# Linear attention and a two-layer MoE block on one core: seven chunk pairs by block products instead of four, weights streamed from DRAM, a recorded instruction order

## The chip, the cores and the metric

The kernel runs on one core of one Trainium2 chip. The metric is the device time of one execution in microseconds (us), median of several runs. The engines are named as the profile names them: PE (TensorE, matmuls), PEld (its weight loads), DVE (VectorE), ACT (ScalarE), POOL (GpSimd) and SP (SyncE, which issues nearly all DMAs from one queue, in order).

## The reference

```python
# q, k, v: (8, 8, 576, 64); w_phi: (64, 128); w_in: (512, 2048); w_out: (2048, 512)
def phi(x):
    proj = np.einsum('bhsd,df->bhsf', x, w_phi)
    proj = proj - np.max(np.abs(proj), axis=-1, keepdims=True)
    return np.concatenate([np.exp(proj), np.exp(-proj)], axis=-1)
q_p, k_p = phi(q), phi(k)
kv = np.einsum('bhsf,bhsd->bhfd', k_p, v)
z = np.sum(k_p, axis=2)                       # the key sums
num = np.einsum('bhsf,bhfd->bhsd', q_p, kv)
den = np.einsum('bhsf,bhf->bhs', q_p, z)[..., None] + 1e-06
x = (num / den).transpose(0, 2, 1, 3).reshape(4608, 512)
h = np.maximum(x @ w_in, 0.0)
out = (h * h) @ w_out
```

## The kernel before

**Attention.** The 64 heads are handled as 32 pairs of heads. The first six pairs (`early`) run while the weights are prepared; the other 26 go through a pipeline of visits (`visit(i)`, `late(p)`): one visit projects the queries of pair i and the keys of pair i+1, makes K'V of pair i and the numerators of pair i-1. The largest absolute projection of each query and the denominators are reduced over partitions by POOL (`partition_all_reduce`, four per pair). The key sums z are made by DVE in `keys` and `late`: per head one add of halves (512 columns), one add of quarters (256) and one add of the last 64 tokens (256), then per pair a 32x32 block transpose and a reduction (512 each). The result makes a round trip through DRAM (`zd`, `za`).

**MoE.** The 4608 tokens are 18 chunks of 256. The hidden layer is cut into 8 pieces of 256 columns (f), so a chunk takes 8 steps. A step has a first matmul (x times w_in, f16 in two halves, three products per block), relu and squaring on ACT, a split of the square into a high and a low part (`gh`, `gl`; the last subtraction on DVE), and a second matmul with w_out of 12 matmuls with 512 columns. The first matmul of one chunk is 24 matmuls of 256 columns (`moe`, line 1051). Chunks 0 to 9 are done so, mixed into the attention.

**Block products.** The last eight chunks are done as four pairs (`pair`, line 1233): for two chunks at once the product is cut into 2x2 blocks and made with seven block products in place of eight (Strassen's scheme in Winograd's form): 42 matmuls of 256 columns where two ordinary first matmuls have 48. Its price is on DVE: sums of weight blocks (`add_w`), sums of chunk blocks (`add_x`), and in each step four adds on the products in PSUM (line 1248: three of 512 columns, one of 256). In the first pair three of the eight steps are ordinary ones, so 29 steps are block steps. w_in lies in SBUF throughout (`win`), and a ring of seven chunk places holds x; chunks 10 to 12 are spilled to DRAM and read back.

**Order.** Every operation is an entry of a plan with its engine, cost, predecessors, buffers and rank. A list scheduler (`Plan.order`, with ranks from a table) computes when each would start and writes the program out in that order; an operation that may run on several engines goes to the one that is free first. At run time each engine runs its own list in order and waits on semaphores.

Of the kernel before, what the change touches and what calls it, by code (L numbers as in the profile page):

```python
# [37 lines left out]
RING = 7 * T  # L38
# [7 lines left out]
LEAD = 36.0  # L46
STEP = 1.4
EARLY = 6
BANKS = 5
STAY = 6.0  # L50
LATER = 2.0
BEHIND = 0.0
MOVED = 70.0
CHANGE = 0.18
RA, RQ, RZ = 1.3, 0.4, 0.3
WARM = 8
FILL_TO = 125.0
PAIRED = 10
PLAIN = 3
SPILLED = (10, 11, 12)  # L60
PAIRS = ((13, 14), (15, 16), (17, 10), (11, 12))
TAIL = LEAD + (STEP - 1.0) * PAIRED * NFP

# [22 lines left out]
class Plan:  # L86
# [11 lines left out]
    def __init__(self):  # L98
        self.ops = []
        self.bufs = {}  # L100
        self.single = set()

# [8 lines left out]
    def close(self):  # L111
# [18 lines left out]

        for (tag, n), mine in users.items():
            if tag in self.single:
                first = mine[0]
                first.after += [a for op in mine[1:] for a in op.after if a not in mine and not self.leads(first, a)]
        self.users = {key: len(mine) for key, mine in users.items()}

    def leads(self, first, op):
        seen, todo = set(), [op]
        while todo:
            x = todo.pop()  # L140
            if x is first:
                return True
            for a in x.after:
                if a.n not in seen:
                    seen.add(a.n)
                    todo.append(a)
        return False

    def improve(self):

        some = [op for op in self.ops if -50.0 < op.rank < MOVED]
        assert 2 * len(some) == len(RANKS)
        for n, op in enumerate(some):
            i, j = (DIGITS.index(x) for x in RANKS[2 * n:2 * n + 2])
            op.rank = (90 * i + j - 3000) * 0.05
        return self.order()

    def order(self):
        for op in self.ops:
            op.start = op.end = None  # L160
            op.next, op.left = [], 0
            op.after = [a for a in {id(a): a for a in op.after}.values() if a is not op]
            op.behind = [a for a in op.behind if a not in op.after and a is not op]
        for op in self.ops:
            for a in op.after + op.behind:
                a.next.append(op)
                op.left += 1
# [8 lines left out]
        def alone(op):  # L176
            return [key for key in op.uses if key[0] in self.single]
# [13 lines left out]
        for op in self.ops:  # L191
            if not op.left:
                release(op)
# [1248 lines left out]
```

## Time and profile before

| | before |
|---|---|
| time, median of 3 runs | 1020.16 us (1019.26 to 1021.61) |
| span of the profiled execution, first to last instruction | 1018.5 us |
| PE busy | 999.8 us (98%) |
| DVE busy | 763.2 us (75%) |
| ACT busy | 680.5 us (67%) |
| POOL busy | 361.2 us (35%) |
| moved by DMA | 77.34 MB, mean 76 GB/s |

The profiled execution is known by its span alone: 1018.5 us, 1.7 us under the median of the runs, and what lies around the span is taken as those 1.7 us. A busy PE is read with care, since matmuls overlap: the time that one costs is read from the distance of starts, not from its length.

### The profile page before, as it was taken

To read this page: it belongs to the slowest core of one execution; us is meant where nothing else is said; L and a number is where in the kernel's file an instruction comes from. 1 tells how busy PE (TensorE), PEld (TensorE's weight loads), DVE (VectorE), ACT (ScalarE), POOL (GpSimd) and SP (SyncE) were. 2 spreads that over 40 slices of the span, in tenths; PEclk is the share of its full clock that TensorE was granted. 3 is DMA by queue.
4 is the path that set the end of the run, shared out by engine and by line. 5 is a ranking of instruction groups with operands and counts; after the bars stand their busy time and mean duration, and the time that the engine had idled before them with its cause. 6 is when DMAs were issued, how large, how long until landed. Compare 5 with 4: busy or idle time off the path is not lost.

```text
span 1018.5 us, 19261 instructions
## 1 busy us (share of the span) xinstructions
PE 999.8 (98%) x7632; PEld 694.6 (68%) x7713; DVE 763.2 (75%) x1221; ACT 680.5 (67%) x1206; POOL 361.2 (35%) x138
## 2 busy tenths in 40 slices
PE   8999999999999999999999999999999999999998
PEld 4657776776666667666767666666776767677675
DVE  5899878798878989777879888798888447343432
ACT  6989886777777787686777867776555445435444
POOL 2433356364456555475375646563000000000000
PEclk9999999999999999999999999999999999999999
DMA  9754323132322233233324212110002001000001
GB/s 355 282 186 135 122 81 94 39 110 73 85 60 81 75 93 93 60 82 81 107 80 111 83 48 69 41 41 22 13 2 83 1 1 49 14 1 21 22 1 42
DMA packets 94914, 77.34 MB, mean 76 GB/s; under 512 B 58088, under 2 KB 72424, under 8 KB 92776
## 3 DMA queue, kind: packets, MB, share of 16 engines
q1 hardware_dynamic: 94536, 75.59, 24.6%
q8 instruction: 60, 0.98, 0.4%
q10 hardware_dynamic: 288, 0.52, 0.1%
q14 instruction: 30, 0.25, 0.1%
HBM read 61.16 MB, written 14.78 MB: 75 GB/s over the span
## 4 chain that ended last, share of the span: by engine, by line
PE 90%; DVE 3%; DMA 3%; ACT 2%; issue 1%; SPq 0%; DVEq 0%; ACTq 0%
PE po L1088 27%; PE ph L1051 21%; PE pp L1233 7%; PE pz L669 4%; PE pv L1088 4%; PE pn L1088 4%; PE ph L1233 3%; PE pn L904 3%; PE pn L884 2%; PE pp L611 2%; PE pv L904 2%; PE pz L1233 2%; PE pz L674 1%; PE pv L669 1%; PE pz L892 1%
## 5 line engine op out<-in xcount | busy, mean ns | idle before, releaser
L1051 PE MATMUL ph<-ring,win 128*128 128x256 f16 x2064 | 240.4, 273 | 0.8 <-ACT r L1060 0.8
L1051 PEld LDWEIGHTS <-win 128*128 128x128 f16 x2064 | 195.3, 98 | 47.0 <-issue 24.8
L982 POOL PARTITION_ALL_REDUCE mx<-pt x52 | 121.6, 2339 | 122.7 <-ACT pt L335 84.3
L1088 PE MATMUL po<-wh,gh 128*128 128x512 f32 x448 | 143.8, 442 | 0.0
L1003 POOL PARTITION_ALL_REDUCE rb<-rb x26 | 96.5, 3712 | 112.0 <-DVE rb L1000 95.6
L1265 ACT ACTIVATE qe<-qe,cw 128x512 f32<-128x512 f32 x58 | 41.4, 715 | 112.5 <-DVE qe L1248 112.5
L1088 PE MATMUL po<-wl,gl 128*128 128x512 bf16 x448 | 115.1, 379 | 0.0
L331 DVE TENSOR_TENSOR gl<-r,gh 128x512 bf16<-128x512 f32 x86 | 87.5, 1018 | 31.7 <-ACT r L1070 30.7
L1003 POOL PARTITION_ALL_REDUCE ds<-ds x26 | 98.7, 3797 | 25.2 <-DVE ds L1000 24.5
L1088 PE MATMUL po<-wl,gh 128*128 128x512 bf16 x375 | 101.5, 379 | 4.9 <-issue 1.6
L1088 PEld LDWEIGHTS <-gl 128*128 128x128 bf16 x576 | 56.4, 98 | 68.0
L1088 PEld LDWEIGHTS po<-wh,gh 128*128 128x128 f32 x448 | 84.6, 189 | 25.9
L1248 DVE TENSOR_TENSOR qe<-pp,qe 128x512 f32<-128x512 f32 (+1 forms) x87 | 52.3, 602 | 61.3 <-PE pp L1233 59.5
L1060 ACT ACTIVATE r<-ph,cw 128x512 f32<-128x512 f32 x86 | 58.7, 683 | 51.0 <-PE ph L1051 49.3
L331 DVE TENSOR_TENSOR gl<-qe,gh 128x512 bf16<-128x512 f32 x58 | 40.1, 691 | 65.7 <-ACT qe L1070 65.6
L1088 PEld LDWEIGHTS <-gh 128*128 128x128 bf16 x576 | 52.3, 98 | 50.7 <-issue 8.9
L633 ACT ACTIVATE e<-e 128x512 f32<-128x512 f32 x64 | 40.0, 625 | 32.3 <-DVE e L630 32.3
L1233 PEld LDWEIGHTS <-win 128*128 128x128 f16 x522 | 48.8, 98 | 14.2 <-issue 7.8
L1068 ACT ACTIVATE gh<-r 128x512 fp32r<-128x512 f32 x86 | 54.1, 629 | 5.7 <-PE pv L1088 2.0
L1070 ACT ACTIVATE r<-r 128x512 f32<-128x512 f32 x86 | 54.3, 631 | 2.7
L650 DVE TENSOR_TENSOR es<-e 128x512 f32<-128x512 f32 x52 | 46.3, 890 | 4.5 <-ACT e L635 4.3
L669 PE MATMUL pz<-e,v 128*64 128x256 f32 x416 | 49.3, 379 | 0.0
(286 smaller groups left out, 1970.4 us busy)
## 6 DMA issues: line engine op xcount, KB each, us to landing
v<-in_vp_dram SPq DMA_DIRECT2D x32, 320.0 KB, 4.1
k<-in_kp_dram SPq DMA_DIRECT2D x32, 288.0 KB, 4.1
q<-in_qp_dram SPq DMA_DIRECT2D x32, 288.0 KB, 3.4
rb<-rd SPq DMA_DIRECT2D x64, 144.0 KB, 3.1
out_dram<-o SPq DMA_DIRECT2D x34, 256.0 KB, 2.1
td<-kvs SPq DMA_DIRECT2D x26, 128.0 KB, 2.6
kz<-td SPq DMA_DIRECT2D x26, 128.0 KB, 2.9
spill<-ring SPq DMA_DIRECT2D x6, 256.0 KB, 2.9
```

The costliest lines, as they stand in the source:

```text
L331: eng.tensor_tensor(out=out_, in0=a, in1=b_, op=ALU.subtract)
L669: PE.matmul(out=to[64 * h:64 * h + 64, 0:256], lhsT=v_[p][:, t, h, :], rhs=e_[2 * p + h][:, t].rearrange("p s f -> p (s f)"), start=t == 0 ...
L904: PE.matmul(out=to[64 * h:64 * h + 64, :], lhsT=kz_[n][:, 128 * s_ + 64 * h:128 * s_ + 64 * h + 64], rhs=qe_[2 * n + h].rearrange("p (s x) ...
L982: o = P.add("POOL", par_us(S), lambda n=n, h=h: G.partition_all_reduce(mx_[n], pt_[p][:, h, :], channels=128, reduce_op=bass_isa.ReduceOp. ...
L1003: o = P.add("POOL", 3.6, lambda y=y: G.partition_all_reduce(y(), y(), channels=128, reduce_op=bass_isa.ReduceOp.add), [o], [home], R(RQ + ...
L1051: PE.matmul(out=ph[:, j, :], lhsT=win[w][:, t, 128 * ff:128 * ff + 128], rhs=at_ring(c, x, t), start=k == 0, stop=k == 3 * KT - 1)
L1060: o = P.add("ACT", act_us(512, 1), lambda: A.activation(out=r_[n], in_=ph_[bank], func=AF.Relu, scale=cw[:, f, 0:1]), [g1], [("ph", bank), ...
L1068: sq = P.add("ACT", act_us(512), lambda: A.activation(out=gh_[n], in_=r(), func=AF.Square), after, use + [("gh", n)], Q)
L1070: o = P.add("ACT", act_us(512), lambda: A.activation(out=r(), in_=r(), func=AF.Square), [sq], use, Q, other=[("DVE", 0.70, lambda: V.tenso ...
L1088: PE.matmul(out=bank(i), lhsT=x[:, j, 128 * i:128 * i + 128], rhs=w[:, j, :], start=turn + j + s == 0, stop=(turn, j, s) == (NFP - 1, 1, 2))
L1233: PE.matmul(out=to, lhsT=fl(x, *al)(k), rhs=fr(y, *ar)(k), start=n == 0, stop=n == 5)
L1248: V.tensor_tensor(out=to, in0=a, in1=b, op=ALU.add)
```

## The change

1. **Seven pairs.** Chunks 0 to 3 stay ordinary; chunks 4 to 17 are seven pairs, each with eight block steps (`step`). That is 56 block steps in place of 29 and 32 ordinary first matmuls in place of 86.
2. **w_in streamed.** Once scaled, the pieces of w_in are stored to DRAM (`wd`), and so are the sums of their blocks, which are made once, early (`ahead`). Each block step loads its piece and its block sums again, 0.5 MB each, into one of two buffers (`weights`). The room in SBUF goes to the temporaries, and the ring has eight places; nothing is spilled.
3. **One of two chunks put away.** In the first six pairs the step's second matmul is made for the first chunk alone. `gh` and `gl` of the second chunk go to DRAM (`put_away`) and are read back for eight second matmuls after the pair's steps (`take_back`). Those steps use the PSUM banks pn and pv, which the attention uses too.
4. **Key sums.** Per head one DVE reduction over 1024 columns with `apply_transpose`, and per pair one over 256; the results go through DRAM and one more small reduction. The subtraction for the last 64 keys moves from DVE into two ACT activations with a bias.
5. **Order.** Ranks and scheduler are gone. A table `ORDER` holds the place of each operation and a string `WAYS` the engine of those that have a choice; the code still computes start times, which now only place the filling matmuls.

```diff
-RING = 7 * T
+RING = 8 * T
-PAIRED = 10
-PAIRS = ((13, 14), (15, 16), (17, 10), (11, 12))
+PAIRED = 4
+PAIRS = [(c, c + 1) for c in range(PAIRED, NCH, 2)]
+MID = 6
...
     def order(self):
+        assert 2 * len(self.ops) == len(ORDER)
+        place = {}
         for op in self.ops:
...
+            place[op.n] = 90 * i + j
+        several = [op for op in self.ops if len(op.ways) > 1]
+        for op, way in zip(several, WAYS, strict=True):
+            op.take(list(op.ways)[int(way)])
+        order = sorted(self.ops, key=lambda op: place[op.n])
...
-        for h in range(0 if p < EARLY else 2):
-            n = 2 * p + h
-            o = P.add("DVE", dve_us(512), lambda n=n: V.tensor_tensor(
-                out=es_[p][:, 512:1024], in0=e_[n][:, 0:2].rearrange("p t s f -> p (t s f)"),
-                in1=e_[n][:, 2:4].rearrange("p t s f -> p (t s f)"), op=ALU.add),
...
+            def fold(src, col, k, after, use, rank):
+                sums[p].append(P.add("DVE", dve_us(256 * k), lambda: V.tensor_reduce(
+                    out=col(), in_=src().rearrange("p k (b x) -> p k b x", x=32), op=ALU.add, axis=AX.X, apply_transpose=True),
+                    [after], [use, ("z4", p)], rank))
...
+    def weights(f, rank):
+        b = in_pair["step"] = in_pair.get("step", 1) ^ 1
+        o = P.add("SP", 0.45, lambda: SP.dma_start(wo_at(b), wd_[f][0]), [w_stored[f]] + read_o[b], [WO[b]], rank, land=2.4, xfer=1.8)
+        if f in s_stored:
+            s = P.add("SP", 0.45, lambda: SP.dma_start(ws_at(b).rearrange("p k n x c -> p k (n x c)"), wd_[f][1]), s_stored[f] + read_s[b], [WS[b]], rank, land=2.4, xfer=1.8)
+            read_o[b], read_s[b] = [], []
+            return b, [o, s]
...
+    def step(cs, k, turn, f, n, m):
...
+        b, w_ready = weights(f, m - 5.0)
...
+        pa = P.add("PE", 0.66, lambda: product(banks[0]()[:, 0, :], "a11", "b11"), after, keys[0] + reads, m)
...
+        pb = P.add("PE", 1.31, two(1, ("a12", "b21"), ("s2", "t2")), [pa], keys[1] + reads, m + 0.01)
+        cb_ = P.add("DVE", dve_us(512), lambda: plus(r()[:, 0:4:3, :], banks[1](), wide(r()[:, 1, :])), [ca, pb], keys[1] + [rt], Q - URGENT)
+        pc = P.add("PE", 1.31, two(2, ("s3", "t3"), ("s1", "t1")), [pb], keys[2] + reads, m + 0.02)
...
+        pd = P.add("PE", 1.31, two(3, ("a22", "t4"), ("s4", "b22")), [pc], keys[3] + reads, m + 0.03)
+        cd = P.add("DVE", dve_us(512), lambda: plus(r()[:, 1:3, :], banks[3](), r()[:, 1:3, :]), [pd, c22], keys[3] + [rt], Q - URGENT)
...
+    def put_away(n, k, f, g, rank):
+        def work():
+            SP.dma_start(gd_[k % 2][f][0], gh_[n].bitcast(F32))
+            SP.dma_start(gd_[k % 2][f][1], gl_[n])
...
+        for j in range(NFP):
+            done = step(cs, k, j, j, n, m)
+            second(n, cs[0], v, j, j, done[0], m + 2.5, po)
+            if mid:
+                put_away(n + 1, k, j, done[1], m)
             else:
-                for i in range(2):
-                    n = v * NFP + 2 * j + i
-                    moe(cs[i], f, j, n, TAIL + n, po[i])
+                second(n + 1, cs[1], v + 1, j, j, done[1], m + 3.5, later)
```

In a block step the bank `ph` holds the first of the seven products and, as a second tile, the last two; the copy `ca` and the add `cd` free it.

The order on DVE, before, for one attention pair in the middle of the program. The es rows are the key sums (three adds per head, transpose, reduction), e the exponentials of the keys, gl the low part of a square.

```order
L655 TENSOR_TENSOR es_3627<-es_3627 128x256
L660 TENSOR_TENSOR es_3627<-es_3627,et_3662 64x256
L650 TENSOR_TENSOR es_3627<-e_3618 128x512
L331 TENSOR_TENSOR qe_3699<-pt_3592,mx_3660 128x576
L655 TENSOR_TENSOR es_3627<-es_3627 128x256
L660 TENSOR_TENSOR es_3627<-es_3627,et_3662 64x256
L1000 SCALAR_TENSOR_TENSOR rb_3721<-qe_3651,zc_3519,pp_3701 128x576
L966 STREAM_TRANSPOSE es_3627<-es_3627 128x512
L331 TENSOR_TENSOR gl_3727<-r_3716,gh_3719 128x512
L967 TENSOR_REDUCE z_8_3757<-es_3627 128x4x4
```

And after the change, at a like place. L1167 are the adds on the products in PSUM (pn, pv, ph) of block steps, w_1 the two temporaries of a step, L580 the new key sums.

```order
L1167 TENSOR_TENSOR w_1_4086<-pv_4254,w_1_4086 128x512
L1167 TENSOR_TENSOR w_1_4086<-pv_4254,w_1_4086 128x256
L1167 TENSOR_TENSOR w_1_4086<-ph_4273,w_1_4086 128x512
L877 STREAM_TRANSPOSE kvs_4317<-pz_4292 128x256
L249 TENSOR_TENSOR gl_4319<-w_1_3621,gh_4271 128x512
L570 TENSOR_REDUCE kmt_4334<-pz_4292 128x1
L249 TENSOR_TENSOR gl_4354<-w_1_3621,gh_4290 128x512
L1167 TENSOR_TENSOR w_1_3621<-pn_4337,w_1_3621 128x2x256
L1167 TENSOR_TENSOR w_1_3621<-pv_4356,w_1_3621 128x512
L1167 TENSOR_TENSOR w_1_3621<-pv_4356,w_1_3621 128x256
L580 TENSOR_REDUCE z_9_4235<-e_3458 128x2x4x4
```

The adds of the key sums have left DVE's list, and adds that read PSUM stand among the attention's operations, which before they did only after the attention's end.

SP's list before, in the later part of the attention: small transfers of the attention (den, rd, rb, td, kz, zd, za) and loads of q, k and v.

```order
L1005 DMA den_5848<-rb_5791 64x1x9
L971 DMA zd_5855<-z_16_5850 128x16
L972 DMA za_5873<-zd_5855 128x4x4
L1005 DMA den_5848<-ds_5832 64x1x9
L821 DMA rd_5909<-rc_5905 128x9
L604 DMA q_5924<-in_qp_dram 128x576
L603 DMA k_5928<-in_kp_dram 128x576
L566 DMA v_5934<-in_vp_dram 128x640
L954 DMA td_5936<-kvs_5930 128x2x128
```

And after the change, at a like place. `wd` are the streamed weights and their block sums, `gd` the parts that are put away.

```order
L1091 DMA w_1_3921<-wd_0_88 128x2048
L1093 DMA w_1_4026<-wd_1_89 128x2048
L524 DMA k_6869<-in_kp_dram 128x576
L1223 DMA gd_0_0_98<-gh_6783 128x512
L1224 DMA gd_0_1_99<-gl_6871 128x512
L878 DMA td_6898<-kvs_6888 128x2x128
L890 DMA zd_6914<-z_17_6758 128x72
L881 DMA kz_6962<-td_6898 128x8x32
L754 DMA rb_6527<-rd_6804 64x576 x2
```

The streamed loads and the parts put away now stand in the same queue as the attention's small transfers. The order also gives the counts that the prediction uses. On PE, 768 rows of ordinary first matmuls are left of 2064, and the block products grow from 1218 to 2352; second matmuls (1728) and attention keep their counts. On SP, 112 loads of 0.5 MB are added, and 96 transfers each way for what is put away.

## Rows read from the trace of the kernel before

**Rows 1.** The page, parts 1 and 2: busy time, and busy tenths in 40 slices.

```profile
PE 999.8 (98%) x7632; PEld 694.6 (68%) x7713; DVE 763.2 (75%) x1221; ACT 680.5 (67%) x1206; POOL 361.2 (35%) x138
DVE  5899878798878989777879888798888447343432
```

**Rows 2.** Windows: us, busy us (and instructions) of each engine, granted clock, DMA.

```profile
83.00:703.00 620.00, 616.15 (x4766) 429.71 (x4813) 525.70 (x828) 461.95 (x839) 331.54 (x114) 1.00 0.29 80
703.00:1014.00 311.00, 307.78 (x2015) 217.82 (x2046) 171.91 (x271) 148.06 (x237) 3.40 (x1) 1.00 0.05 19
```

**Rows 3.** Waits of PE from 83 us on: us in total, times, longest.

```profile
PE po L1088 <- issue: 1.6, 10, 0.2
PE pp L1233 <- DVE qe L1248: 0.9, 1, 0.9
PE ph L1051 <- ACT r L1060: 0.8, 1, 0.8
```

**Rows 4.** Timeline of PE, two places: start us, us, what.

```profile
87.40 2.79 PE L1051 MATMUL ph<-ring,win 128*128 128x256 f16 x24
90.03 1.03 PE L1088 MATMUL po<-wl,gh 128*128 128x512 bf16 x3
...
92.69 0.50 PE L1051 MATMUL ph<-ring,win 128*128 128x256 f16 x3
...
722.39 0.83 PE L1233 MATMUL pz<-ring,win 128*128 128x256 f16 x6
...
729.64 0.83 PE L1233 MATMUL pz<-ring,win 128*128 128x256 f16 x6
```

**Rows 5.** Groups of DVE instructions, all shapes apart: busy us, mean ns, idle before.

```profile
L650 DVE TENSOR_TENSOR es<-e 128x512 f32<-128x512 f32 x52 | 46.3, 890 | 4.5 <-ACT e L635 4.3
L655 DVE TENSOR_TENSOR es<-es 128x256 f32<-128x256 f32 x52 | 39.0, 750 | 1.1
L660 DVE TENSOR_TENSOR es<-es,et 64x256 f32<-64x256 f32 x52 | 33.4, 643 | 1.8
L966 DVE STREAM_TRANSPOSE es<-es 128x512 f32<-128x512 f32 x26 | 18.4, 707 | 0.4
L967 DVE TENSOR_REDUCE z<-es 128x16 f32<-128x512 f32 x26 | 17.8, 683 | 0.5
L640 DVE TENSOR_TENSOR et<-pz,kmt 128x128 f32<-128x128 f32 x26 | 7.4, 286 | 0.7
L331 DVE TENSOR_TENSOR gl<-r,gh 128x512 bf16<-128x512 f32 x86 | 87.5, 1018 | 31.7 <-ACT r L1070 30.7
L1248 DVE TENSOR_TENSOR qe<-pp,qe 128x512 f32<-128x512 f32 x58 | 40.0, 690 | 60.3 <-PE pp L1233 59.5
L1248 DVE TENSOR_TENSOR qe<-pp,qe 128x256 f32<-128x256 f32 x29 | 12.3, 424 | 1.0
L1000 DVE SCALAR_TENSOR_TENSOR rb<-qe,zc,pp 128x576 f32<-128x576 f32 x26 | 21.0, 807 | 1.1 <-ACT pp L998 0.8
```

**Rows 6.** Lines 331 and 1003 alone: min/median/max ns, first and last start.

```profile
L331 DVE TENSOR_TENSOR gl<-r,gh x86: 650/692/3050, 89.0 to 722.2; 128x512 bf16<-128x512 f32 x86
L331 DVE TENSOR_TENSOR gl<-qe,gh x58: 680/692/694, 731.5 to 1008.8; 128x512 bf16<-128x512 f32 x58
...
L1003 POOL PARTITION_ALL_REDUCE rb<-rb x26: 3592/3593/4123, 146.6 to 696.9; - x26
```

**Rows 7.** DVE's busiest 20 us in the attention, from windows.

```profile
380.00:400.00 20.00, 19.95 (x158) 13.82 (x158) 19.58 (x31) 14.13 (x26) 11.78 (x5) 1.00 0.31 86
```

**Rows 8.** DMA issues: KB each, median us from issue to landing.

```profile
raw7i<-in_w_in_dram SPq DMA_DIRECT2D x1, 1024.0 KB, 4.8
raw4i<-in_w_in_dram SPq DMA_DIRECT2D x1, 1024.0 KB, 11.0
```

**Rows 9.** SP's own waits, 83 to 703 us.

```profile
SPq L1005 <- POOL rb L1003: 91.4, 23, 8.2
```

More of the change, by code (lines that the diff above doesn't have):

```diff
@@ L129, in close @@
                 op.after.append(first)
[L131 to L134, printed above, removed]
         self.users = {key: len(mine) for key, mine in users.items()}
[L137 to L156, printed above, removed]
     def order(self):
+        assert 2 * len(self.ops) == len(ORDER)
+        place = {}
         for op in self.ops:
[L160 to L167, printed above, removed]
+            i, j = (DIGITS.index(x) for x in ORDER[2 * op.n:2 * op.n + 2])
+            place[op.n] = 90 * i + j
[3 more added lines that the diff above has]
+        order = sorted(self.ops, key=lambda op: place[op.n])
         free = dict.fromkeys(self.HOP, 0.0)
-        waiting = {e: [] for e in self.HOP}
-        ready = {e: [] for e in self.HOP}
-        holder, open_at, parked = {}, {}, {}
+        holder, open_at = {}, {}
         mode, moved = WHOLE, 0.0
@@ L174, in order @@
         users = dict(self.users)
-        def alone(op):
-            return [key for key in op.uses if key[0] in self.single]
-        def release(op):
-            least = max([open_at.get(tag, 0.0) for tag, n in alone(op) if holder.get(tag) != n] + [a.start + 0.001 for a in op.behind], default=0.0)
-            for eng in op.ways:
-                at = least
-                for a in op.after:
-                    at = max(at, a.there + (self.HOP[a.eng] if a.eng != eng or a.land else 0.0))
-                second = eng != next(iter(op.ways))
-                heapq.heappush(waiting[eng], (at + LATER * second, op.rank + BEHIND * second, op.n))
@@ new lines, in order @@
+        for op in order:
+            e, (us, _, lock) = op.eng, op.ways[op.eng]
+            op.start = max([free[e]] + [a.there + (self.HOP[a.eng] if a.eng != e or a.land else 0.0) for a in op.after if a is not op]
+                           + [a.start + 0.001 for a in op.behind if a is not op])
+            alone = [key for key in op.uses if key[0] in self.single]
+            for tag, n in alone:
+                assert holder.get(tag, n) == n
+                if tag not in holder:
+                    op.start = max(op.start, open_at.get(tag, 0.0))
+            op.end = op.start + us
@@ L229, in order @@
                 else:
-                    op.end += min(lock, max(0.0, locked["POOL"] - t))
+                    op.end += min(lock, max(0.0, locked["POOL"] - op.start))
                     locked[e] = op.end
@@ L1351, in tile_kernel @@
     pool_next.after += pool_prep
+    ring1.after += [op for op in P.ops if v_key(NP) in op.uses]
     for op in P.ops:
@@ L1375, in tile_kernel @@
         if free:
-            fills.append((t0, len(P.ops), lambda tag=free[0], n=n, count=int(0.6 * (t1 - t0) / 0.214): zeros(tag, n, count)))
+            fills.append((t0, lambda tag=free[0], n=n, count=int(0.6 * (t1 - t0) / 0.214): zeros(tag, n, count)))
     with tc.manual_schedule():
-        for _, _, fn in sorted([(op.start, op.n, op.fn) for op in order] + fills, key=lambda x: x[:2]):
-            fn()
+        for op in order:
+            while fills and fills[0][0] <= op.start:
+                fills.pop(0)[1]()
+            op.fn()
```

679 lines of the change are left out of this document (361 added, 318 removed).

## The prediction, made before the changed kernel ran

> **What bounds the kernel now.** I read the page's busy times first, then windows, then PE's waits. PE is busy for 98% of the span [rows 1], so the question is where it is not. Three stretches answer it: until the first first-matmul (83 us), the attention with ordinary chunks (83 to 703), and the pairs (703 to 1014). In the second PE is busy for 616 of 620 us, in the third for 308 of 311, at a full granted clock [rows 2]; all its named waits behind 83 us come to 3.3 us [rows 3]. So PE's work is the time: a matmul taken away behind 83 us is worth its full price, as long as nothing else comes to limit.
>
> The other engines tell how far that is. DVE is next: 526 of 620 us in the attention, 85%, but only 172 of 311, 55%, in the pairs [rows 2], and its slices show the same fall [rows 1]. ACT has 462 of 620 and POOL 332; DMA is at 0.29 of its time in the attention and at 0.05 behind it [rows 2]. The change moves DVE's work from the last stretch into the second, where there is least room.
>
> **The change, part by part.**
>
> *Products.* The order gives 1296 ordinary matmuls less and 1134 block products more: 162 fewer matmuls of 256 columns, six for each of 27 more block steps. Their price is the distance of starts: 24 ordinary ones take from 87.40 to 90.03, 2.63 us, or 0.1096 us each. A block step of 42 and the second matmul behind it take from 722.39 to 729.64, 7.25 us; a second matmul takes 2.66 (from 90.03 to 92.69), so the block step takes 4.59 us, 0.1093 us each [rows 4]. Both forms run at one rate, so the gain is 162 x 0.1093 = 17.7 us. Nothing bounds it from above but PE's idle time; that the matmuls read other buffers doesn't alter their form. The three filling matmuls that vanish stand in gaps and count nothing.
>
> *Key sums.* What goes is 46.3 + 39.0 + 33.4 + 18.4 + 17.8 = 154.9 us of DVE, and the 7.4 us of the subtraction that ACT takes over: 162.3 us [rows 5]. What comes is 52 reductions of 1024 columns and 26 of 256, transposing as they read; no row shows such a form. From below: a reduction of 512 takes 683 ns, and one of 1024 at the same rate about 0.683 + 512/0.96 ns = 1.22 us. From above: a transpose and a reduction one behind the other, 1.24 + 1.22 = 2.46 us. With 0.44 us (0.44 to 0.88) for the small ones that is 75 to 151 us. [...]
>
> *DVE in the attention.* By the order 40 of the 56 block steps now begin before the last visit's numerators, with 32 ordinary first matmuls and 104 second ones; before there were 83 and 81. PE's stretch then grows to 620 - 51 x 2.63 + 40 x 4.59 + 23 x 2.66 = 731 us. DVE's load in it: 526 - 162 + 75 for the sums; 40 steps of three adds of 512 and one of 256, 40 x (3 x 0.690 + 0.424) = 100 us [rows 5]; sums of chunk blocks for five pairs and of weight blocks, made in halves, priced at those rates by their columns, 46 + 47 us, of which some 15 were there before; 29 more gl, 30 us; copies, squares and output scalings that WAYS gives to DVE, about 40. That is 687 of 731 us, 94%. Before it was 85%, and in the busiest 20 us of the attention DVE had 19.58 and PE still 19.95 [rows 7]. So 94% is no bound by itself.
>
> *What a late DVE now costs.* Before, an ordinary step's bank was freed by ACT (the relu), and a late DVE met only second matmuls, which lag. Now four adds of DVE stand between the block step's banks and the next one: `ca` and `cd` free ph. By the order 22 of the 40 steps have no more than one second matmul and a short attention piece between their last product and the next first one, about 2.66 us of cover. DVE does run late by more: of 86 gl in the attention the median is 692 ns, the mean 1018 and the longest 3050, while behind 703 us, when POOL has stopped, the longest is 694 [rows 5, 6]. POOL's reductions hold it. [...] The rows agree: the transposes, reductions and operations with a PSUM operand show means near their price (707, 683, 807 ns), the adds of two SBUF inputs do not (890, 750, 643) [rows 5].
> The mean surplus of gl, 0.326 us, is 14% of the greatest, 2.36 us. If 14% of 160 adds have a full stall ahead of them, 22 hits, each costs 3.05 - 2.66 = 0.39 us of PE where there is no more cover, in 22 of 40 steps: 22 x 0.39 x 22/40 = 5 us. Bounds: nothing, where the order keeps such operations out of POOL's way; and 0.39 us for each of POOL's 104 reductions, 41 us. I take 5, since surplus like this was rare in the rows.
>
> *Streamed weights.* A buffer comes free when step g-2 has its products and is needed when step g begins: one block step between two second matmuls, 2.66 + 4.59 + 2.66 = 9.9 us. Two loads of 0.5 MB are as much as one of 1 MB, which landed in 4.8 us on a quiet queue and in 11.0 at the crowded start [rows 8]. The loads of 40 steps and the parts put away are some 70 MB in 731 us, 96 GB/s on top of the 80 there; at the ratio of that row the queues' share goes from 0.29 to about 0.64 [rows 2]. That leaves room, so I count nothing; at the start's 11.0 us it is 1.1 us a step, 62 us for 56. The parts put away and read back (0.375 MB each) are covered in the same way by two second matmuls, 5.3 us, and three buffers.
>
> *Order and the rest.* At run time both kernels hold a fixed order, so a table in place of a scheduler costs nothing by itself. ACT loses the relus of 54 first matmuls and gains two a block step; with 75% in the attention it has room. Sum, for the median: 1020.2 - 17.7 + 5 = **1007 us** (its profile: 1006 us of span).
>
> **The rivals.**
> 1. *DVE becomes the bound.* If the new reductions take two passes, 76 us are added to 687: 763 of 731. If the adds are held like gl, it is 160 x 0.326 = 52 us more, 739. A DVE that is never more than 98% busy, as in its best 20 us [rows 7], then needs 779 or 754 us for the stretch in place of 731, 48 or 23 more on 1002 (the sum without stalls): 1050 or 1025 us, around 1035 for a case between. For: the load is the highest of any stretch. Against: the rows of single-source operations. It ends slower than before from about 736 us of DVE work on (1022 less 1002 is 20 us; 98% of 751).
> 2. *Loads behind a waiting SP.* SP works in order, and its DMAs wait in it: those of line 1005 for POOL 23 times, up to 8.2 us [rows 9]. A load queued behind such a hold lands 8.2 + 4.8 = 13.0 us after its buffer is free, 3.1 us late. Six such holds eat the gain; one in four steps gives 14 x 3.1 = 43 us, 1045 us. Against: most holds are shorter, and the load's place can be ahead of them.
> 3. *Better than the sum.* No stalls at all, 1002, and a part of the 11.6 us that PE idles outside the two stretches (18.7 in all, less 3.9 and 3.2) closed by another packing: 998 us.
> 4. *The gain is eaten.* DVE's stalls come to 15 to 20 us, half of their upper bound: 1018 to 1022, no change.
>
> **How the numbers follow.** A measurement of this kernel can tell 0.2%, 2 us, from no change (three runs spread over 2.4 us). My forecast (1000 to 1017) has 0.54, rival 3 has 0.13, rival 4 0.08, rival 1 0.17 and rival 2 0.08. Faster is the first two, 0.67; same 0.08; slower 0.25. The range from 996 to 1034 leaves out rival 2, the upper half of rival 1 and the end of rival 3: nearly 2 in 10. The likeliest case's own range is 1000 to 1017.
>
> **What would show it.** Right: 162 fewer matmuls at the same distance of starts; L580 rows near 1.22 us for 1024 columns; DVE at 90 to 95% up to the last visit, and that visit's numerators at about 83 + 731 = 814 us; PE's waits behind 83 us at some 8 us, mostly on L1167. Wrong: L580 above 2 us, DVE at 98% over hundreds of us, PE waiting for DMA of w, or waits of a us or more at many block steps.

## The result: slower by half a per cent, with the matmuls saved as forecast

Six runs of the changed kernel took 1026.37 us in the median (1021.14 to 1028.83), six of the kernel before beside them 1019.91; the ratio is 1.0052 [1.0029, 1.0074]. A second set (below) gave 1025.96 and 1.0058 [1.0046, 1.0070]. The forecast was 1007 and faster. The profiled run took 1026.95 us, with a span of 1025.1.

First the page of the changed kernel: busy times, and DVE and the clock in 40 slices.

```profile
PE 999.6 (98%) x7548; PEld 679.8 (66%) x7548; DVE 799.8 (78%) x1407; ACT 604.3 (59%) x1131; POOL 357.1 (35%) x144
DVE  5898789899798788988789888777897776672443
PEclk9899999999999999999999999999999999999999
```

PE is as busy as before [rows 1], though 162 of its matmuls are gone. (The trace of the kernel before lacks 81 rows of PE, so its 999.8 us is a little low; the twin introduced below has all of them, and 1006.3.) So either its matmuls became dearer, or its clock fell. The new forms are not dearer. PE's timeline shows a block step between two second matmuls, and the groups of DVE the new key sums:

```profile
433.11 0.83 PE L1161 MATMUL ph<-ring,w 128*128 128x256 f16 x6
...
437.71 1.03 PE L993 MATMUL po<-wl,gh 128*128 128x512 bf16 x4
...
440.37 0.83 PE L1161 MATMUL ph<-ring,w 128*128 128x256 f16 x6
```
```profile
L249 DVE TENSOR_TENSOR gl<-w,gh 128x512 bf16<-128x512 f32 x112 | 80.6, 727 | 23.9 <-ACT w L975 23.1
L580 DVE TRANSPOSE_TENSOR_REDUCE z<-e 128x32 f32<-128x1024 f32 x52 | 64.0, 1233 | 3.8 <-ACT e L556 3.2 <-DMA zd<-z 0.7
L1167 DVE TENSOR_TENSOR w<-ph,w 128x512 f32<-128x512 f32 x56 | 38.4, 686 | 9.8 <-PE ph L1161 7.3 <-DVE w L1167 0.5
L580 DVE TRANSPOSE_TENSOR_REDUCE z<-et 128x8 f32<-128x256 f32 x26 | 11.1, 428 | 0.0
```

The step takes 4.60 us and the second matmul behind it 2.66, as in [rows 4]. The transposing reduction takes 1233 ns and the small one 428; the adds on PSUM stand at 686. The gl of block steps have a mean of 727 over the whole run; up to 835 us, in the attention, it is 742 for those 80 and 828 for the 32 of ordinary steps, where the kernel before had 1018 [rows 5]. The DMA view has the streamed loads (KB each, median us to landing):

```profile
w<-wd SPq DMA_DIRECT2D x112, 512.0 KB, 4.4
```

Where the time went shows in windows by stretch (us, busy us of each engine, granted clock, DMA share, GB/s). Ahead of them, for comparison, the same windows of a twin of the kernel before (its order, with the new reductions in the key sums, run e13 below):

```profile
0.00:80.00 80.00, 73.84 (x810) 45.49 (x814) 64.63 (x120) 67.31 (x127) 26.05 (x24) 1.00 0.72 262
80.00:150.00 70.00, 69.87 (x579) 50.88 (x579) 58.02 (x87) 61.91 (x101) 27.41 (x14) 1.00 0.39 123
150.00:280.00 130.00, 129.34 (x1000) 88.13 (x997) 89.54 (x144) 92.88 (x175) 66.38 (x24) 1.00 0.28 79
280.00:300.00 20.00, 20.00 (x160) 13.56 (x159) 11.21 (x20) 14.22 (x27) 11.57 (x4) 1.00 0.28 69
300.00:900.00 600.00, 597.51 (x4423) 416.27 (x4422) 424.17 (x681) 391.65 (x695) 220.14 (x74) 1.00 0.21 57
900.00:930.00 30.00, 30.00 (x201) 21.22 (x200) 11.65 (x18) 12.88 (x23) 0.00 (x0) 1.00 0.00 1
```

The changed kernel:

```profile
0.00:80.00 80.00, 69.95 (x772) 45.95 (x773) 64.00 (x125) 61.64 (x111) 35.82 (x30) 0.94 0.75 260
80.00:150.00 70.00, 66.30 (x580) 44.51 (x579) 57.48 (x97) 52.26 (x95) 26.53 (x15) 1.00 0.43 127
150.00:280.00 130.00, 128.68 (x999) 87.60 (x998) 116.83 (x209) 90.28 (x177) 73.88 (x25) 1.00 0.44 120
280.00:300.00 20.00, 18.03 (x105) 12.01 (x104) 19.17 (x35) 11.22 (x20) 7.47 (x2) 0.91 0.13 41
300.00:900.00 600.00, 598.05 (x4375) 410.61 (x4373) 484.30 (x851) 351.74 (x669) 213.40 (x72) 1.00 0.66 198
900.00:930.00 30.00, 28.06 (x177) 19.11 (x174) 22.55 (x37) 8.05 (x13) 0.00 (x0) 0.94 0.53 185
```

From 300 to 900 us, where most block steps lie, PE is idle for 1.95 us of 600, less than the twin's 2.49. The loss lies outside. PE's idle time is 10.0 against 6.2 us up to 80, 3.7 against 0.1 up to 150, 1.3 against 0.7 up to 280, 2.0 against 0 up to 300, and 1.9 against 0 at 900 to 930. Behind these gaps the granted clock is low: (1 - clock) x length gives 4.8 + 1.8 + 1.8 us, and nothing in the twin. Together that is some 20 us more than the twin, 12 of idle time and 8 of clock, in these two profiled executions; what the lower clock costs in time follows below.

A second account agrees. Give each matmul its undisturbed distance to the next (0.1093 us for 256 columns, 0.222 for a second matmul, the attention's in the same way) and subtract the sum of those issued from the time: what is left I call the **lag**. It is worked out from all rows of PE in the trace; where a trace lacks some (the runs e5 to e12 lack one matmul in a hundred), they are put in at their pace. Of this work the changed kernel has 971.7 us and the twin 989.4, so 17.7 are saved. Its growth by stretch, twin and changed kernel: up to 80 us 20.9 and 24.4; to 150, 0.1 and 5.7; to 280, 0.9 and 2.8; to 300, -0.2 and 4.0; to 900, 3.8 and 7.1; to 930, 0.2 and 4.2; at the end 0.1 and 0.8. In all some 23 us are lost against 17.7 saved, and the spans differ by 1025.1 - 1019.8 = 5.3.

The stretch up to 80 us needs care, since one execution stands for it. Six profiled executions of kernels with the same instructions up to there (this one, e3, e5, e6, e10, e15) start the first of the ordinary first matmuls between 88.7 us (e15) and 97.3 us (e10), this one at 93.3. The 3.5 us lost up to 80 us lie within that spread.

The page's waits name the places. Waits of PE from 83 us on, us in total, times, longest:

```profile
PE ph L956 <- DVE r L967: 2.3, 3, 1.6
PE pn L725 <- ACT n L253: 1.6, 1, 1.6
PE po L993 <- DVE o L1014: 1.5, 1, 1.5
PE pp L532 <- DVE ds L924: 1.1, 2, 0.6
PE pn L341 <- DVE m L498: 1.1, 1, 1.1
PE pz L818 <- DMA q<-in_qp_dram: 0.8, 1, 0.8
PE pp L1161 <- DVE w L1167: 0.5, 1, 0.5
```

Half a us falls on the adds of block steps, behind 900 us, and none on the loads of streamed weights. And this is what one wait looks like, in PE's timeline at 284 us and in the slices around it:

```profile
282.88 1.28 PE L993 MATMUL po<-wh,gh 128*128 128x512 f32 x4
285.71 0.50 PE L956 MATMUL ph<-ring,w 128*128 128x256 f16 x3 [1.55 <-DVE r L967]
286.63 4.01 PE L956 MATMUL ph<-ring,w 128*128 128x256 f16 x21 [0.42 <-DVE ring L1075]
290.43 1.18 PE L993 MATMUL po<-wl,gh 128*128 128x512 bf16 x4
```
```profile
280.00:285.00 5.00, 4.16 (x19) 2.27 (x17) 4.62 (x10) 4.17 (x7) 1.54 (x1) 1.00 0.32 99
285.00:290.00 5.00, 3.87 (x22) 2.81 (x23) 4.93 (x5) 0.00 (x0) 5.00 (x2) 0.73 0.03 11
```

Twenty-one matmuls that take 2.3 us at their pace took 3.8 (286.63 to 290.43). PE had been idle for 2 us, and the granted clock of the slice behind is 0.73. The two waits took 2 us, and the slower matmuls behind them 1.7 more. The same happens at 916 us (1.5 us for an output scaling on DVE; the clock is 0.88 from 915 to 920 us and 0.78 from 920 to 925).

But that 1.7 is not the price of the clock. A second profiled execution of the same kernel (e5) has the same two waits, and the clock stays up:

```profile
286.49 0.50 PE L956 MATMUL ph<-ring,w 128*128 128x256 f16 x3 [1.55 <-DVE r L967]
287.41 2.45 PE L956 MATMUL ph<-ring,w 128*128 128x256 f16 x21 [0.42 <-DVE ring L1075]
293.61 2.78 PE L956 MATMUL ph<-ring,w 128*128 128x256 f16 x24 [1.10 <-ACT r L965]
```
```profile
285.00:290.00 5.00, 3.09 (x26) 2.54 (x27) 4.93 (x6) 0.73 (x2) 5.00 (x2) 1.00 0.20 68
```

The 21 matmuls are done sooner, and then PE waits 1.10 us for the next relu. From the second matmul ahead of the hole to the first matmul behind it (282.88 to 293.24, in e5 283.66 to 293.61) it is 9.95 us in place of 10.36: here the lower clock cost 0.4 us. At 916 us no further wait stood behind, and the clock, 1.00 there in e5 too, is worth 1.6 us (914.44 to 924.63 is 10.19 us, in e5 915.08 to 923.65 is 8.57).

### The profile page after: what moved, and what is told of

The parts are those of the page before. It is cut to its first block, busy times and chain, and to the rows that moved or that the text cites. A ratio compares the mean times of both kernels' runs of the same rounds, so it can differ in the third digit from the quotient of the medians.

```text
span 1025.1 us, 19857 instructions
## 1 busy us (share of the span) xinstructions
PE 999.6 (98%) x7548; PEld 679.8 (66%) x7548; DVE 799.8 (78%) x1407; ACT 604.3 (59%) x1131; POOL 357.1 (35%) x144
## 4 chain that ended last, share of the span: by engine, by line
PE 80%; DVE 7%; DMA 5%; issue 3%; ACT 2%; POOL 2%; SPq 1%; POOLq 0%; DVEq 0%; ACTq 0%
PE po L993 30%; PE ph L1161 10%; PE pn L1161 6%; PE pv L1161 6%; PE ph L956 6%; PE pz L594 4%; PE pn L830 3%; PE pp L1161 2%; PE pn L809 2%; PE pp L532 2%; PE pv L830 2%; DMA q<-in_qp_dram 1%; DMA rb<-rd 1%; PE pz L599 1%; PE pv L993 1%
## 5 line engine op out<-in xcount | busy, mean ns | idle before, releaser
L1161 PEld LDWEIGHTS <-w 128*128 128x128 f16 x2352 | 224.3, 98 | 48.4 <-issue 20.7
L993 PE MATMUL po<-wl,gh 128*128 128x512 bf16 x544 | 141.0, 381 | 1.8 <-DVE o L1014 1.5
L1212 ACT ACTIVATE w<-w,cw 128x512 f32<-128x512 f32 x112 | 78.6, 714 | 107.7 <-DVE w L1167 107.7
L973 ACT ACTIVATE gh<-w 128x512 fp32r<-128x512 f32 x112 | 69.9, 625 | 62.4 <-PE po L993 30.0
L249 DVE TENSOR_TENSOR gl<-w,gh 128x512 bf16<-128x512 f32 x112 | 80.6, 727 | 23.9 <-ACT w L975 23.1
L956 PE MATMUL ph<-ring,w 128*128 128x256 f16 x768 | 91.1, 276 | 2.8 <-DVE r L967 2.3
L956 PEld LDWEIGHTS <-w 128*128 128x128 f16 x768 | 73.5, 99 | 22.9 <-issue 12.1
L1161 PE MATMUL ph<-ring,w 128*128 128x256 f16 x624 | 85.6, 273 | 0.0
L1161 PE MATMUL pv<-w,w 128*128 128x256 f16 x576 | 70.7, 273 | 0.3 <-ACT pt L253 0.3
L580 DVE TRANSPOSE_TENSOR_REDUCE z<-e 128x32 f32<-128x1024 f32 x52 | 64.0, 1233 | 3.8 <-ACT e L556 3.2
L1167 DVE TENSOR_TENSOR w<-pv,w 128x512 f32<-128x512 f32 x96 | 53.1, 553 | 10.2 <-PE pv L1161 8.1
L249 DVE TENSOR_TENSOR qe<-pt,mx 128x576 f32<-128x576 f32 x52 | 45.6, 878 | 10.1 <-POOL mx L906 5.5
L1167 DVE TENSOR_TENSOR w<-pn,w 128x512 f32<-128x512 f32 x48 | 32.9, 686 | 23.3 <-PE pn L1161 14.1
```

What stands on the lines that cost most here:

```text
L249: eng.tensor_tensor(out=out_, in0=a, in1=b_, op=ALU.subtract)
L580: sums[p].append(P.add("DVE", dve_us(256 * k), lambda: V.tensor_reduce(out=col(), in_=src().rearrange("p k (b x) -> p k b x", x=32), op=AL ...
L956: PE.matmul(out=ph[:, j, :], lhsT=w_[f][0][:, w, t, 128 * j:128 * j + 128], rhs=at_ring(c, x, t), start=k == 0, stop=k == 3 * KT - 1)
L973: sq = P.add("ACT", act_us(512), lambda: A.activation(out=gh_[n], in_=r(), func=AF.Square), after, use + [("gh", n)], Q)
L993: PE.matmul(out=bank(i), lhsT=x[:, j, 128 * i:128 * i + 128], rhs=w[:, j, :], start=turn + j + s == 0, stop=(turn, j, s) == (NFP - 1, 1, 2))
L1161: PE.matmul(out=to, lhsT=fl(x, *al)(k), rhs=fr(y, *ar)(k), start=n == 0, stop=n == 5)
```

## The experiments

Sixteen kernels ran. Theory A: PE's work is the time, and the gain is lost in a few waits outside the block steps and in the clock behind them. Theory B: a late DVE costs PE in the block steps. Theory C: the added traffic holds up the attention's transfers.

**e1: relus and scalings on ACT.**

```diff
+        P.on_act.append(o)                 # moe: relu
...
+            if v < NCH - 2:                # store: scaling
+                P.on_act.append(o)
```

> The six relus of ordinary first matmuls and the output scalings of the chunks before the last pair that the table gives to DVE go to ACT; nothing else is changed. Theory A (the gain is lost in a few waits of PE, by 300 us and at the last pair's start, and in the clock that falls behind them): the waits of PE on L967 (1.55 us at 284) and on L1014 (1.50 us at 916) vanish and the clock stays up there; the lag of PE behind its paced work grew by 4 us at each place, so 8 us less than the changed kernel, about 1018 us. Theory B (a late DVE costs PE a little in many block steps): both places are two of many, less than 3 us gained, 1023 to 1026. Theory C (the streamed weights and the parts put away hold up other transfers): no change, 1026.

1021.01 us, 1.0013 [1.0000, 1.0026]: 5 us better than the changed kernel. The part at 916 us came out: the lag grows by 1.7 us there in place of 4.2 (2.6 in e5's profile, where the clock stayed up). The part at 284 didn't; the wait stayed, under another name:

```profile
281.46 0.49 PE L959 MATMUL ph<-ring,w 128*128 128x256 f16 x3 [1.43 <-ACT r L968]
282.50 3.78 PE L959 MATMUL ph<-ring,w 128*128 128x256 f16 x21 [0.56 <-DVE ring L1081]
```

On ACT the relu stands behind operations that themselves wait for DVE (2.39, 0.46 and 0.30 us at 275.9, 277.1 and 279.2 us; the relu starts at 280.73). What else was gained lies up to 150 us, where the lag is 4 us smaller than in the first profile; how much of that the relus at 100 to 160 us did, and how much is the spread of the start, this run doesn't tell.

**e2: filling matmuls at seven waits.**

```diff
+            if op.n in MORE:
+                tag, count = MORE[op.n]
+                zeros(tag, 100 + op.n, count)
+MORE = {159: ("pv", 10), 12: ("pz", 7), 285: ("pv", 4), 382: ("pp", 7), 577: ("pn", 5), 2142: ("pn", 14), 3457: ("pv", 14)}
```

> Filling matmuls, whose result nobody reads, stand ahead of seven operations at which PE waited in the changed kernel (at 4.5, 21, 40, 87, 148, 284 and 916 us), for about as long as the wait; the waits themselves stay. Theory A, the clock's part: the granted clock was 0.66 to 0.95 in the slices behind these gaps, (1 - clock) x length is about 10 us over the run; most of the 8 us that stand above the kernel before should come back, 1018 to 1020 us, with a mean clock of 0.998. If the lower clock is only beside the loss and costs nothing: no change, 1026, or some us more from fills that end late.

1020.52 us, 1.0002 [0.9992, 1.0012]: 5.4 us come back from matmuls that compute nothing. Over all runs the mean granted clock is 0.999, and 0.994 in those of e5 (0.991 to 0.997); 0.005 of 1025 us is about as much as came back. So the clock behind the gaps is a cost of its own in the sum of them, apart from the waits. At 284 us it is not: the clock stayed at 1.00, but the waits were still there, and the lag grew by 3.5 us, hardly less than 4.

**e3: streamed loads of 16 columns.**

```diff
+        n = 1024 if whole else 16          # whole: the first two steps
+        SP.dma_start(to[:, :, 0:n], of[:, :, 0:n])
```

> From the third block step on each load of streamed weights moves 16 of 1024 columns (all 112 loads and their waits stay in SP's list, 55 MB of traffic go; the products then read old weights). Theory C (traffic): DMA's share falls from 0.6 to 0.9 behind 340 us to about 0.3, waits for DMA go, and the time falls by 5 us or more, to 1020 or less. Theory A: the loss lies ahead of the first streamed loads or at 916 us, where PE waited for DVE, so no change, 1024 to 1027. Theory B: no change either.

1023.46 us, 1.0031 [1.0019, 1.0044]: 2.5 us below the second set of the changed kernel. With DMA's share from 300 to 900 us at 0.43 in place of 0.66, the lag grows by 5.9 us there, against 7.1. Traffic is worth 1 to 3 us, not the loss.

**e4: seven matmuls fewer per block step.**

```diff
-                    PE.matmul(..., start=n == 0, stop=n == 5)
+                    if n < 5:
+                        PE.matmul(..., start=n == 0, stop=n == 4)
```

> The last of six matmuls of every block product is left out (the lowest term of the sum): 7 of 42 in each of the 56 block steps, 392 in all; everything else stays. Theory A (from 300 us on PE's work is the time): 392 x 0.1093 = 43 us less, 982 to 986 us. Theory B (DVE sets the pace of the block steps): DVE's work stays, it was 84% busy from 300 to 800 us, so a part of the 43 us at most, 20 or less, 1006 or more. Theory C (the loads set it): likewise 1006 or more.

990.81 us, 0.9714 [0.9698, 0.9730]: 35 us less of 43. PE is the bound of the block steps, for more than four fifths of a saving of this size; the other engines then begin to show (DVE 507 of 600 us, PE idle for 10).

**e5: the changed kernel again.** The file is the same but for an empty line.

> The changed kernel, unaltered, for a second set of runs beside the other three of this group: its single runs spread from 1021 to 1029 us before, so its median is needed on the same footing as the edits of some us. Theory A and every other: 1022 to 1027 us; a median at 1021 would say that the filling matmuls and the moved scalings of the first two experiments gained nothing.

1025.96 us (1025.20 to 1027.51): the footing for the differences given here. Its profile, with a mean clock of 0.996 where the first had 0.991, is the second execution read above.

**e6: sums made ahead for one piece of eight.**

```diff
+            one = lambda fn: fn if f == 0 else lambda: None
-            o = P.add("DVE", 0.84, fill, ...)
+            o = P.add("DVE", 0.84, one(fill), ...)
```

and in the same way for `block_sums` and the last subtraction.

> The sums of weight blocks that are made ahead (DVE, 60 to 296 us) are computed for the first piece alone; for the other seven the three DVE operations of each half are left out (the ACT copy and the transfers stay, the stored sums are old ones), some 40 us of DVE. Theory A1 (between 80 and 300 us PE waits because DVE has this work on top of the attention): the lag of PE behind its paced work, which grew by 12 us from 80 to 300, grows by 5 or less; 1018 to 1020 us. Theory A2 (the early waits are the attention's own chain, each step's operation waiting for the one before it, with few ordinary matmuls to put between): the lag grows by 9 or more, less than 3 us gained.

1021.95 us, 1.0016 [1.0002, 1.0031]: 4 us gained. The hole at 284 us is gone (the lag grows by 0.6 from 280 to 300, against 4), but from 80 to 280 it grows by 9.2, as much as in the changed kernel. So A1 holds for the hole and A2 for the rest. DVE is still slow there, with POOL busy for 7.2 of the 20 us from 280 on: the gl of 281.7 us takes 3.06 us in place of 0.69, and the relu behind it makes PE wait 0.5 us.

**e7 and e9: key sums twice, and not at all.**

```diff
+                def twice():
+                    for _ in range(2):
+                        V.tensor_reduce(out=col(), ..., apply_transpose=True)
```
```diff
-lambda: V.tensor_reduce(out=col(), ..., apply_transpose=True)
+lambda: V.memset(col(), 1.0)
```

> Each transposing reduction of the key sums is made twice, one behind the other: 78 more DVE instructions, 64 + 11 = 75 us, as if the new form had cost 2.46 us. It is the upper bound of the prediction's price, and shows how near DVE is to being the bound. Theory B (a late DVE is what PE pays for in the block steps): 15 us or more on top, 1040 and above. Theory A (PE is the bound from 300 to 900 us, DVE at 84% there has room): 6 us or less on top, 1025 to 1032.

> The changed kernel with its 78 reductions for the key sums left out: a fill of 72 columns in all stands in their place (the denominators are then wrong), so DVE loses some 70 us, the counterpart of the run with twice the reductions, which cost 32 us for 75. If DVE's load is a bound beside PE's (the slope goes on downwards): 10 us or more less than the changed kernel, 1016 or less. If only more DVE work than the order was made for hurts (a kink at today's load): 4 us or less gained, 1022 to 1026.

Twice: 1058.16 us, 1.0376 [1.0362, 1.0389], 32 us more for 75 us of DVE. Not at all: 1023.44, 1.0026 [1.0011, 1.0042], 2.5 us less for some 70. So there is a kink somewhere above today's load. Windows from 300 to 900 us, twice and then not at all (PE's columns lack about one matmul in a hundred):

```profile
300.00:900.00 600.00, 577.75 (x4124) 394.25 (x4177) 523.92 (x887) 341.56 (x652) 213.33 (x73) 0.99 0.62 187
```
```profile
300.00:900.00 600.00, 594.34 (x4318) 411.35 (x4375) 450.40 (x848) 351.10 (x668) 213.77 (x72) 1.00 0.66 198
```

With DVE at 87% the lag grows by 32.7 us in this stretch, at 75% by 7.3; in the changed kernel, at 81%, it grows by 7.1. Theory B fails for the changed kernel. A few per cent above it a late DVE does cost PE, though not in the block steps alone: of the named waits of that stretch 8 us stand at block products and 9 at the attention's matmuls. An upper-end price of the key sums would have been fatal.

**e8, e12, e14, e16: a mended order.** All do the whole work: filling matmuls, scalings on ACT, and single operations at another place of the table.

```diff
+        for n, behind in MOVE.items():
+            place[n] = place[behind] + 0.5
+MOVE = {577: 2015, 584: 2027, 2142: 2131}               # e8
+MOVE = {577: 2015, 584: 2027}                           # e12
+MOVE = {577: 2015, 584: 2027, 2137: 2119}               # e14
+MOVE = {577: 2015, 584: 2027, 2137: 2119, 2241: 2142}   # e16
```

> Five of the filling places, the output scalings on ACT, and three of PE's operations set one place later, behind a matmul group that was ready (the gather at 149 us and the key projection at 164 us each behind a second matmul, the ordinary first matmul at 286 us behind the next second one); all of the work is done. Theory A: the gains of the first two experiments add up in part and 3 to 5 us of waits at 149, 164 and 286 us go: 1014 to 1018 us, faster than the kernel before. If the waits only move on to the next operation: 1020 to 1022.

> The mended order without the move that made a new wait of 3.6 us at 286 us: filling matmuls at six places, output scalings on ACT, the gather at 149 us and the key projection at 164 us each behind a ready second matmul; all of the work is done. By the lag of the first mended run, less the 1.8 us that it lost more than the others at 280 to 300 us: about 2 us better than that one, 1017 to 1019 us. If the places taken out only let the next wait come forward: 1020 to 1021.

> The mended order of the changed kernel once more (filling matmuls, output scalings on ACT, two PE operations one place later), and in place of the filling matmuls at 284 us the relu that PE waits for there is moved up in DVE's list, ahead of the chunk writes, the denominators and the sums made ahead between which it stood (from 272.4 to 268.1 us of the plan). All of the work is done. If that wait and the clock behind it were worth the 3 to 4 us by which the lag grew there: 1015 to 1017 us. If what DVE does later then makes PE wait instead: 1018 to 1020.

> The mended order with both of these moves: filling matmuls at five places, output scalings on ACT, gather and key projection one place later, relu early, the fill of the sum behind the matmul. All of the work is done. If the hole at 284 us closes: 1015 to 1017 us, faster than the kernel before by 3 us or more. If not: 1018 to 1021, as the other mended runs.

In this order: 1020.59 (1.0012 [1.0001, 1.0022]), **1018.75** (0.9981 [0.9968, 0.9994]), 1020.58 (0.9999 [0.9990, 1.0008]) and 1020.79 us (1.0011 [1.0002, 1.0020]). Five to seven us come back; e12 alone is below the kernel before, by 0.2%. Its waits at 149 and 164 us are gone. e12 alone of the four also has filling matmuls at 284 us. No attempt closed the hole there: from 280 to 300 the lag grows by 5.3, 2.7, 4.2 and 3.8 us in these four (in e12 a part of the hole, some 0.7 us, lies ahead of 280).

**e10: all that ACT can do goes to ACT.**

```diff
+            if "ACT" in op.ways and 400 < place[op.n] < 3480:
+                op.take("ACT")
```

> Every operation between some 90 and 920 us that the table gives to DVE and that ACT can do (squares, copies, halves of the chunk sums, output scalings, relus) goes to ACT, at the same place of the order: about 60 us from DVE (80%) to ACT (59%). If DVE's load is what PE pays for from 100 us on: 5 to 10 us gained, 1016 to 1021. If it is the order of single operations that hurts: moved operations wait behind others on ACT as the relu at 284 us did, and nothing is gained, 1024 to 1030.

1025.88 us, 1.0055 [1.0033, 1.0076]: nothing gained, with DVE at 439 of 600 us from 300 to 900 (484 in the changed kernel). That agrees with e9.

**e11 and e13: the kernel before with the new key sums, in a new and in its old order.** The same work in both; in e13 the plan keeps the old costs and dependencies. In e11 six operations that may run on more than one engine also went to another (ACT has 1200 instructions, 1206 in e13).

```diff
-            o = P.add("DVE", dve_us(512), lambda n=n: V.tensor_tensor(...), [exps[p][h]] + folded, ..., lock=4.0)
+            o = P.add("DVE", 0.0, lambda: None, [exps[p][h]], ...)                            # e11
+            o = P.add("DVE", dve_us(512), lambda: None, [exps[p][h]] + folded, ..., lock=4.0) # e13
```

and in the same way for the others: in both, the last add of each head becomes a transposing reduction of 1024 columns, the transpose one of 256, the reduction a small one.

> The kernel before with the change's key sums alone: per head one transposing reduction of 1024 columns, per pair one of 256 and a small one in place of the three adds, the transpose and the reduction (some 75 us of DVE less; the sums land in another order, so the denominators are wrong). Its list scheduler makes the order anew. The prediction's reading (PE's work is the time before, DVE's 85% in the attention costs nothing): 1017 to 1021 us. If DVE's load costs PE there too: 1012 or less.

> The same edit of the kernel before as in the run that gave 1068.8 us (the change's key sums, in another order of sums), but the planned costs and the dependencies of the old operations are kept, so that the list scheduler puts every instruction of PE, ACT, POOL and SP where it stood before, and on DVE only the kind of the key sums' own instructions differs. If the 48 us came from the order that the scheduler made of new costs with ranks that belong to the old ones: 1017 to 1021 us, no loss and no gain, since PE's work is the time. If the transposing reductions themselves hold something up: 1040 or more.

New order: 1068.77 us, 1.0468 [1.0447, 1.0489]. Old order: 1021.22, 1.0009 [1.0000, 1.0018]. The new order's greatest wait of PE, and the window where PE is idle most:

```profile
PE pp L611 <- DVE ds L995: 13.7, 3, 9.3
```
```profile
330.00:360.00 30.00, 19.22 (x149) 13.00 (x145) 21.80 (x37) 18.58 (x37) 17.53 (x7) 0.77 0.35 94
```

The order, with those six, is worth 48 us here, and DVE was no busier (694 us in all, in e13 692). In the old order some 70 us less of DVE than in [rows 1] gained nothing, as the prediction's reading of the kernel before had it.

**e15: two moves at 284 us alone.**

```diff
+MOVE = {2137: 2119, 2241: 2142}
```

> The changed kernel with two operations moved by a place or a few, all of the work done: the relu of 284 us stands ahead of the chunk writes in DVE's list, and the fill of the next sum made ahead stands behind the ordinary first matmul of 284 us instead of ahead of it (both use the second part of the ring: the matmuls read chunk 3 there, the sum uses the last place as a temporary; in the run before, with the relu early, PE stood 2.68 us behind that fill). If the shared tile is what PE waits for there: no wait of a us at 276 to 290 us, the lag grows by 1 us or less instead of 4, and 2 to 4 us are gained, 1022 to 1024. If DVE is simply too late there: the wait moves to the next matmul, 1025 to 1027.

1025.96 us, 1.0068 [1.0054, 1.0081]: nothing. PE's first wait of the hole, which would fall at 280 us in this run, went, and the next first matmul waited for 3.9. DVE's timeline shows by what, and ACT's who stood behind it:

```profile
274.44 0.94 DVE L251 TENSOR_TENSOR ring<-ring 128x128 f32<-128x128 f32 x3
...
282.06 3.40 DVE L251 TENSOR_TENSOR ring<-ring 128x128 f32<-128x128 f32 x3
```
```profile
285.49 0.63 ACT L1081 ACTIVATE ring<-ring 128x512 f16<-128x512 f32 x1 [5.74 <-DVE ring L251]
...
286.89 0.67 ACT L967 ACTIVATE r<-ph,cw 128x512 f32<-128x512 f32 x1
```
```profile
287.62 4.45 PE L958 MATMUL ph<-ring,w 128*128 128x256 f16 x24 [3.92 <-ACT r L967]
```

The three subtractions of a sum made ahead take 0.94 us while POOL is idle, and 3.40 while it reduces (POOL is busy for all of 282 to 285.5 us). In the changed kernel itself they take 0.95 us at 280.2, with POOL idle, and 3.40 at 287.3, with POOL busy. Why they take longer beside POOL was not shown. ACT's copy of the sum waits for them (5.74 us), the relu stands behind that copy, and PE waits for the relu (3.92 us). Whichever link was moved, the next one in the chain stood there. e6, which takes the sums away, is the one that closes the hole.

## Why the prediction was wrong

The step that failed is **Order and the rest**: "At run time both kernels hold a fixed order, so a table in place of a scheduler costs nothing by itself". True of the form, it took for granted that an order as tight as the old one stands in the table. That the order by itself can be worth 48 us is shown by e11 against e13. What stood in its place in the changed kernel: of the 23 us lost, 20 lie outside the stretch from 300 to 900 us, in waits and in the clock behind them, for which the sum had no term. 5 to 7 us of these are shown to come back by other places and filling matmuls (e1, e2, e12), and some 4 are the sums made ahead (e6, in part the same us). Whether a better order of the same work would give back the rest isn't shown.

Point by point:

- *Products* was right: 17.7 us of work saved, both forms at their old pace. A saving in block steps is worth four fifths or more of its price (e4).
- *Key sums* was right at the lower end: 1233 and 428 ns against 1.22 and 0.44 us. The 0.96 columns a ns in its estimate is the pace of the adds on PSUM in [rows 5], 690 less 424 ns for 256 columns; the new form's own is 1233 less 428 ns for 768 columns, 0.95. That the transpose adds nothing, as the sum's 75 us has it, was the author's estimate and stood in no row of the kernel before; the new rows come to 64.0 + 11.1 = 75.1 us.
- *DVE in the attention* was mis-sized without harm: forecast 687 of 731 us to 814 us, measured 634 of 752 to 835, 84% in place of 94%. The step's conclusion, that 94% is no bound by itself, rested on one stretch of 20 us and doesn't hold: at 87% over 600 us DVE already cost PE some 26 us (e7).
- *What a late DVE now costs*: the forecast was 5 us. From 300 to 900 us the lag grows by 3.3 us more than the twin's, so the size came near, but by luck: only 0.5 us of PE's waits is on the adds of block steps, where 22 steps at 0.39 us were in question, and 1 of the 3.3 goes with the traffic (e3). What cost PE were the sums made ahead, which the prediction had priced by their columns alone: they stood ahead of the relu at 284 us in DVE's list, and a part of them was slow while POOL reduced (3.40 in place of 0.95 us). Without them 4 us come back; how much of that goes with POOL wasn't taken apart.
- *Streamed weights* was right: loads land in 4.4 us, and no wait of PE in the first profile names them, one of 0.9 us in e5's; without their bytes 1 to 3 us are gained (e3).
- The sum's frame was the second error. It priced PE's stretch from 83 us on as one, with 8 us of waits, mostly on the adds (10.8 us are named there, 0.5 of it on the adds), and carried over the idle time outside it. But the loss is 3.5 us up to 80 (within the spread of that stretch), 5.6 up to 150, 1.9 up to 280, 4.2 up to 300 and 4.0 at 900 to 930. The clock that falls behind a gap had no term at all: it is 8.4 us in the profiled execution and some 4 in e5's.

Of the rivals, none came true as written: DVE didn't become the bound, the streamed loads held PE for 0.9 us at most in the two profiles of the changed kernel, and the stalls of rival 4 are there but small. The lower price of rival 1, 1025 us, meets the measured time by luck: it is for adds held like gl, and they stood at 686 ns, with DVE at 84%.

Left open is the lag of 80 to 280 us: it grows by 1.0 us in the twin, by 8.5 in the changed kernel, and by 5.6 to 9.2 in e6, e9 and e12. It isn't the sums made ahead, nor mostly DVE's load or the traffic. Its waits are links of the early attention's own chain (a gather, denominators, a key projection, 0.5 to 1.9 us each); that the order could hide them was tried at two places only, and left most of it. The part up to 80 us was not taken apart beyond the fills.

## What to carry to other kernels

When PE is busy for 98%, a saving in its steady stretch is real (35 of 43 us in e4), and what decides is whether the rest of the schedule still has no holes; price the first and last stretches by themselves, and each hole with the lower clock behind it, where no other wait stands behind (1.6 us at 916 us, against 0.4 at 284, where one does). Before a kernel whose order is tuned is changed, measure the order apart from the work: the same work in another order, as in e11 and e13, says how much can be lost (48 us here). An engine at 81% can be a few per cent from being the bound: at 87% DVE cost some 26 us (e7).

## What the runs showed that I had not expected

- Matmuls that compute nothing, some 60 of them in seven gaps, made the kernel 5.4 us faster (e2): the granted clock's mean over all runs went from 0.994 (e5) to 0.999.
- Behind the same waits of PE its clock was lower in one execution and not in another: behind 1.55 and 0.42 us at 284 us it was 0.73 in the first profile and 1.00 in e5's, and the two differ there by 0.4 us alone, since another wait took the place of the slower matmuls.
- The transposing reduction takes 1227 to 1233 ns for 1024 columns and 419 to 428 for 256, in the changed kernel and in e13: as much, within 2%, as the prediction's estimate of a plain reduction of 1024 columns from [rows 5] (1.22 us), so by that estimate the transpose costs nothing on top.
- Three subtractions of 128 columns went from 0.94 to 3.40 us beside POOL's reductions, a factor of 3.6.
